# Turning two layer-norm tiles by VectorE and a trip through DRAM instead of by TensorE, at the start of an MLP

## The chip, the core and the metric

The kernel runs on one NeuronCore of a Trainium2 chip, as one launch. The metric is the device time of that launch in microseconds (us); three runs of the kernel before gave a median of 882.88 us. The core has TensorE (PE; its weight loads are shown as PEld), VectorE (DVE), ScalarE (ACT), GpSimd (POOL) and SyncE (SP), which here only issues DMAs. Each engine works through its own queue in the order in which the program was written; semaphores join the queues.

## The reference, cut to what matters

Two layers of a linear attention block followed by an MLP, on 2048 rows of 448 float32 values. Every block reads a layer-normed copy of x and adds its result to x.

```python
def _A_ref(x, wqkv, wo):          # H = 16 heads of Dh = 28
    q, k, v = split(x @ wqkv)
    phi = lambda t: where(t > 0, t + 1, exp(t)) + 1e-6
    pq, pk = phi(q), phi(k)
    kv = einsum("bhsd,bhse->bhde", pk, v);  z = sum over s of pk
    o = (pq @ kv) / (pq . z + 1e-6)
    return o @ wo
def _B_ref(x, w1, b1, w2, b2):    # F = 1792
    return gelu(x @ w1 + b1) @ w2 + b2

for layer in range(2):
    x = x + _A_ref(_layernorm(x), wqkv, wo)
    x = x + _B_ref(_layernorm(x), w1, b1, w2, b2)
```

## The kernel before, in words

The 2048 rows are 16 tiles of 128 rows; four tiles make a block (b = 0 to 3) of the MLP. Precision is kept by splitting every float32 operand into a high part in fp32r and a low part (operand minus high), so each product is three matmuls (high-high, high-low, low-high). The last 64 of the 448 columns share one chunk: its high and low weights lie in the two halves of 128 rows, which is why the last 64 columns of a normed tile are doubled before they are turned.

A layer has these stages.

- **Phase 1** goes over the 16 tiles: layer norm, turning the tile (features onto partitions), splitting, keys (`stage_k`, "psk"), the sum G of key products (`stage_g`), and queries (`stage_q`, "psq", eleven matmuls each), whose positive map is written to DRAM (`pq_d`). Queries run in phase 1 for the tiles below `DEFER`; the others are left for the next stage. Step t makes G of tile t − 1, from the keys' high and low parts kh and kl.
- **The hinge**, between the halves of the layer, is written out by hand in the string `ORDER`, one token after the other. It turns G into the matrix M = (masked kv) · wo (`kv`, `mask`, `m`, `ms`), and brings the first block through the output product: `qz`, `qs`, `tq`, `qq` prepare a tile of queries, `o` multiplies (12 matmuls, "op"), `la` adds the result to x and takes the layer-norm statistics, `lb` normalises ("xm"). Then `T` turns the normed tile by four TensorE transposes into a bank ("tp"), and `x` splits it from that bank into XH (ScalarE) and XL (VectorE). Between these stand the deferred queries: `Q` is a query's matmuls, `Qp` reads it out (two relus, "eq" and "ep", and an exponential on ScalarE, an addition on GpSimd, a store to DRAM on SyncE), and `Qv`, for the last, does the addition on VectorE. A query's result lies in one of two "h" banks, which the MLP's "hp" uses too. The token `pre` issues the four query tiles of the next block and, in layer 0 only, two pieces of the second MLP weight.
- **The MLP** goes over its four blocks with `mlp1` (11 matmuls of 512 columns, "hp", over all four tiles of a block at once), GELU, and `mlp2`; beside each block the next one is prepared as the plans PLAN_0, PLAN_1 and PLAN tell.

The first block's normed tiles are turned by TensorE. The later blocks' are turned without it: `turn` transposes 32 × 32 squares by VectorE's stream transpose into a buffer "sq" that takes two tiles, `store_sq` writes it to DRAM (512 KB), `spread` reads it back with four DMAs of 128 KB each into "sp", so that the squares end up in their places, and `split_t` splits a tile from there.

Layer norm takes statistics on VectorE (bst, bmv, bve), the inverse root on GpSimd (brs), and the normalisation on VectorE again (xm). A buffer ring "S" of five 128 × 1024 buffers holds the staged weights, the parts of M, and the squares. SyncE issues all DMAs in the order of the program text, each when its own waits are over, and what is written behind a waiting DMA waits too.

The string that orders the hinge before:

```python
    ORDER = (
        "Q ld1 z ld0 ld2 qz0 qz1 G gt qs1 Q Qp kv qs0 tq1 Q mask qz2 tq0 qs2 ld3 "
        "m0 qq1 Qp m1 qz3 ms0 qq0 m2 ms1 m3 ms2 tq2 ms3 qs3 o0 la0 qq2 o1 tq3 lb0 la1 qq3 Qp pre "
        "o2 T0 lb1 la2 o3 x0 T1 Q lb2 la3 x1 T2 Q x2 lb3 Qp "
        "T3 x3 Qp Q Qv "
    )
    DEFER = NT - ORDER.split().count("Q")
```

Of the kernel before, what the change touches and what calls it, by code (L numbers as in the profile page):

```python
# [10 lines left out]
F32R = mybir.dt.float32r  # L11
AF = mybir.ActivationFunctionType
OP = mybir.AluOpType
# [9 lines left out]
def linear_attn_mlp_kernel(  # L23
# [12 lines left out]
    pe, act, dve, pool, sp = nc.tensor, nc.scalar, nc.vector, nc.gpsimd, nc.sync  # L36
    x0 = x_in[0]
    y_out = out[0]
    S, D = x0.shape
    F = w1.shape[1]  # L40
# [4 lines left out]
    G = 112  # L45
# [10 lines left out]
    def dram(shape, dt, name):  # L56
        return tc.dram_tile(shape, dt, name=name)
# [13 lines left out]
    def t512(tag, bufs, name, dt=F32):  # L71
        return work.tile([128, 512], dt, name=name, tag=tag, bufs=bufs)

    def f(ap):
        return ap.bitcast(F32)
# [94 lines left out]
    m3 = mask.rearrange("p (h d) -> p h d", d=DH)  # L170
# [15 lines left out]
    def table(func):  # L186

        act.activation(none, tiny, func)
# [13 lines left out]
    def ln_norm(stats, name):  # L202
        xs, mv, rs = stats
        xn = t512("xn", 2, name)
        dve.tensor_scalar(xn[:, :D], xs, mv[:, 0:1], rs, op0=OP.subtract, op1=OP.mult)
        return xn
# [23 lines left out]
    def block(key):  # L230
        if key not in blocks:
            blocks[key] = Block()
        return blocks[key]
# [10 lines left out]
    def split_x(key, j):  # L244
        tp = tps.pop((key, j))
        hi, lo = blocks[key].pieces(j)
        act.copy(hi, tp)
        dve.tensor_sub(lo, tp, f(hi))
# [7 lines left out]
    def half(name):  # L256
        return work.tile([128, 1024], F32, name=name, tag="S", bufs=5)

    def turn(x, key, t):
        x = x[:, :D]  # L260
        if (key, t // 2) not in squares:
            squares[key, t // 2] = half("sq")
        sq = squares[key, t // 2].rearrange("p (m c u n) -> p c m u n", m=4, c=4, n=32)[:, :, :, t % 2]
        dve.transpose(sq[:, :3], x[:, :TL].rearrange("p (c m n) -> p c m n", c=3, n=32))
        dve.transpose(sq[:, 3].rearrange("p (u m) n -> p u m n", u=2),
                      x[:, TL:].rearrange("p (m n) -> p m n", n=32)[:, None].to_broadcast([128, 2, 2, 32]))

    def store_sq(key, h):
        d = stored[key, h] = dram([128, 1024], F32, f"sq_{'_'.join(map(str, key))}_{h}")
        sp.dma_start(d, squares.pop((key, h)))  # L270

    def spread(key, h):
        r = spreads[key, h] = half("sp")
        d = stored.pop((key, h)).rearrange("(i r) (m f) -> m r i f", i=4, m=4)
        for m in range(4):
            sp.dma_start(r[m * 32:(m + 1) * 32].rearrange("r (i f) -> r i f", i=4), d[m])

    def split_t(key, t, hi, lo):

        x = spreads[key, t // 2].rearrange("p (i c u n) -> p u c i n", i=4, c=4, n=32)[:, t % 2]  # L280
        h = hi.rearrange("p (c i n) -> p c i n", c=4, n=32)
        act.copy(h, x)  # L282
        dve.tensor_sub(lo.rearrange("p (c i n) -> p c i n", c=4, n=32), x, f(h))  # L283


    def proj(name, key, j, o=None, cs=range(4)):
# [59 lines left out]
    def background(n, m=NF):  # L346

        for g in bg_wait[:m]:
            bg_wait.pop(0)()
        for _ in range(n):  # L350
            g = next(bg, None)
            if g is not None:
                bg_wait.append(g)


    xns, split, ks = {}, {}, {}
# [79 lines left out]
    def stage_q(l, t):  # L436
        if t is None:
            return
        qo.append((l, t, proj("q", ("a", l, t // 4), t % 4)))
# [7 lines left out]
    def fill_qphi():  # L447

        l, t, o = qo.pop(0)
        e = t512("e", 3, "eq")[:, :D]  # L450
        p = t512("E", 2, "ep")[:, :D]
        act.activation(e, o, AF.Relu, scale=-1.0)
        act.activation(p, o, AF.Relu)
        act.activation(e, e, AF.Exp, scale=-1.0)
        pool.tensor_tensor(e, p, e, op=OP.add)
        sp.dma_start(pq_d[l][t * 128:(t + 1) * 128, :], e)

    def stage_g(l, t, acc):
# [14 lines left out]

    ORDER = (
# [4 lines left out]
    )  # L481
    DEFER = NT - ORDER.split().count("Q")

# [125 lines left out]
    def trans_ms(tr, g):  # L609
        if g == 0:  # L610
            tr.Mh, tr.Ml = [], []
        if g % 2 == 0:
            for n in ("Mh", "Ml"):
                s = work.tile([128, 1024], F32R, name=n, tag="S", bufs=5)
                getattr(tr, n).extend(s[:G, i * D:(i + 1) * D] for i in range(2))
        act.copy(tr.Mh[g], tr.mp[g])
        dve.tensor_sub(tr.Ml[g], tr.mp[g], f(tr.Mh[g]))

# [21 lines left out]
    def load_pq(l, b, j):  # L640
        t = b * 4 + j
        pqt[l, t] = t448(f"W{j}", 1, f"pq{l}_{t}")
        sp.dma_start(pqt[l, t], pq_d[l][t * 128:(t + 1) * 128, :])
# [64 lines left out]
    def o_n(l, b, j):  # L708
        t = b * 4 + j
        xn = xns["m", l, t] = ln_norm(sts.pop(("m", l, t)), f"xm{l}_{t}")  # L710
        if b == 0:
            act.copy(xn[:, D:], xn[:, TL:D])

    def add_bias(l, b, j):
# [5 lines left out]
        transpose_x(xn, xn[:, TL:], ("m", l, b), j)  # L720

    def m_split(l, b, j):
        split_x(("m", l, b), j)


    def q_prep(l, b, j, tr):
# [149 lines left out]
    for l in range(LAYERS):  # L876
        tr = SimpleNamespace(mp={})
        za, acc = phase1(l, tr)
        if l == 0:
            background(0)  # L880
        fill = list(range(DEFER, NT))

        def pre(j):
            for k in range(4):
                load_pq(l, 1, k)
            if l == 0:
                background(2)

        tok_ = SimpleNamespace(
            Q=lambda j: stage_q(l, fill.pop(0)), Qp=lambda j: fill_qphi(), Qv=lambda j: stage_qphi(), G=lambda j: stage_g(l, NT - 1, acc),  # L890
            ld=lambda j: (load_pq(l, 0, j), load_x(l, j)), z=lambda j: trans_z(tr, za), gt=lambda j: trans_gt(tr, acc),
            kv=lambda j: trans_kv(tr), mask=lambda j: trans_mask(tr), m=lambda j: trans_m(tr, j),
            ms=lambda j: trans_ms(tr, j), qz=lambda j: q_z(l, 0, j, tr), qs=lambda j: q_scale(l, 0, j, tr),
            tq=lambda j: q_transpose(l, 0, j), qq=lambda j: q_split(l, 0, j), o=lambda j: o_mm(l, 0, j, tr),
            la=lambda j: o_ln(l, 0, j), lb=lambda j: o_n(l, 0, j), T=lambda j: m_transpose(l, 0, j),
            x=lambda j: m_split(l, 0, j), pre=pre)
        for tok in ORDER.split():
            name, j = tok.rstrip("0123456789"), int("0" + tok.lstrip("abcdefghijklmnopqrstuvwxyzQTG"))
            getattr(tok_, name)(j)
        assert not fill and not qo  # L900
        table(AF.Gelu_apprx_tanh)
        q_z(l, 1, 0, tr)
        mlp1(l, 0, 0)
        trans_chunks(tr)
        for b in range(NB):
            acc = [bank("acc", 4, f"y{j}")[:, :D] for j in range(4)]
            nxt = b + 1 < NB
            if not nxt and l + 1 < LAYERS:
                st_k = stage_square(wqkv[:, D:2 * D])
                st_q = stage_square(wqkv[:, :D])  # L910
                load_to(l + 1, PRE - 1)
            for i in range(NF):
                if i + 1 < NF:
                    mlp1(l, b, i + 1)
                elif nxt:
                    mlp1(l, b + 1, 0)
                if l == 0 and b == 0 and i:
                    background(1, 1)
                if i == NF - 2 and not nxt and l + 1 < LAYERS:
                    table(AF.Exp)  # L920
                if 9 <= i < 13:
                    add_bias(l, b, i - 9)
                if nxt:
                    behind(l, b, i, tr)
                elif l + 1 < LAYERS:
                    if i == 2:
                        split_kq("k", st_k)
                    if i == 5:
                        split_kq("q", st_q)
                    if i in (3, 4, 6, 7, 8):  # L930
                        t = (3, 4, 6, 7, 8).index(i)
                        stage_a(l + 1, t)
                        stage_n(l + 1, t)
                        stage_t(l + 1, t)
                        if t % 2:
                            stage_sp(l + 1, t)
                    if 9 <= i < 13:
                        stage_x(l + 1, i - 9)
                mlp2(l, b, i, acc)
# [28 lines left out]
```

## Time and profile before

| what | value |
|---|---|
| median of three runs | 882.88 us (882.62 to 883.0) |
| the profiled execution: its time | 882.53 us |
| the profiled execution: its span, first to last instruction | 880.8 us |
| instructions in the span | 11686 |
| mean granted TensorE clock in the span | 1.000 |
| VectorE's stream transposes, 128 x 384 and 128 x 128 | 578 and 269 ns each |
| DMAs: HBM read and written | 55.65 MB and 34.08 MB |

The profile is one execution. The page gives the busy time of each engine and the chain of waits that ended last; the timeline gives each instruction with its start in microseconds from the first one, its duration, and in brackets the idle time before it with what ended it. TensorE's matmuls are pipelined: the pace is read from start to start, and the durations overlap. Rows of SyncE ("SPq") are issues; a DMA's landing is told separately, as the time from its issue until its semaphore is complete. The hinge of layer 0 lies at about 107 to 142 us, that of layer 1 at about 539 to 574 us.

### The profile page before, as it was taken

How to read it: one execution, taken by the hardware profiler on the slowest of the kernel's cores; microseconds unless marked ns; L12 is line 12 of the kernel's file. 1: busy time of each engine (PE TensorE's matmuls, PEld its weight loads, DVE VectorE, ACT ScalarE, POOL GpSimd, SP SyncE). 2: the span in 40 equal slices, each digit the busy share in tenths (PEclk: the TensorE clock that was granted, in tenths of full speed). 3: DMA queues.
4: the chain of work that ended last, by engine and by line, in shares of the span. 5: the costliest groups of instructions: out<-in, count | busy, mean ns of one | idle time of the engine just before them, and what ended most of it. 6: DMA issues, size and time to landing. Idle time of an engine off the chain costs nothing.

```text
span 880.8 us, 11686 instructions
## 1 busy us (share of the span) xinstructions
PE 872.7 (99%) x4190; PEld 774.4 (88%) x4190; DVE 486.2 (55%) x946; ACT 345.6 (39%) x607; POOL 219.0 (25%) x251
## 2 busy tenths in 40 slices
PE   8999999999999999999999999999999999999998
PEld 7899988888888888888899999888888888888887
DVE  6878585658455543225567866755574473432112
ACT  5577645323223232333355664442232133223221
POOL 4456632325012102011222333220220140140000
PEclk9999999999999999999999999999999999999999
DMA  6377715624413403051146452143332323110001
GB/s 177 114 214 235 217 43 170 192 81 144 132 59 102 157 0 96 1 178 48 48 133 198 150 148 95 63 158 95 103 115 90 112 74 132 48 49 34 9 1 42
DMA packets 62762, 93.71 MB, mean 106 GB/s; under 512 B 8816, under 2 KB 57968, under 8 KB 62704
## 3 DMA queue, kind: packets, MB, share of 16 engines
q1 hardware_dynamic: 62704, 92.97, 33.7%
q8 instruction: 33, 0.54, 0.3%
q14 instruction: 25, 0.20, 0.1%
HBM read 55.65 MB, written 34.08 MB: 102 GB/s over the span
## 4 chain that ended last, share of the span: by engine, by line
PE 96%; DVE 2%; ACT 1%; DMA 1%; issue 0%; SPq 0%; POOL 0%; ACTq 0%; DVEq 0%; POOLq 0%
PE y L770 10%; PE y L768 10%; PE y L769 10%; PE hp L751 9%; PE hp L750 9%; PE hp L752 9%; PE hp L754 3%; PE hp L753 3%; PE G L465 2%; PE G L466 2%; PE G L464 2%; PE psk L295 2%; PE psq L293 2%; PE psk L294 2%; PE psk L293 2%; PE psq L295 2%
## 5 line engine op out<-in xcount | busy, mean ns | idle before, releaser
L760 DVE TENSOR_TENSOR gl<-g,gh 128x512 fp32r<-128x512 f32 x112 | 82.6, 737 | 299.5 <-ACT gh L759 299.5
L756 ACT ACTIVATE g<-hp,b1s 128x512 f32<-128x512 f32 x112 | 77.0, 688 | 406.4 <-PE hp L754 406.4
L770 PE MATMUL y<-w2h,gl 128*128 128x448 f32 x448 | 163.8, 366 | 0.0
L769 PE MATMUL y<-w2l,gh 128*128 128x448 f32 x448 | 163.8, 366 | 0.0
L768 PE MATMUL y<-w2h,gh 128*128 128x448 f32 x448 | 163.7, 366 | 0.0
L751 PE MATMUL hp<-XH,w1l 128*128 128x512 f32 x336 | 131.7, 392 | 0.0
L750 PE MATMUL hp<-XH,w1h 128*128 128x512 f32 x336 | 131.3, 391 | 0.0
L752 PE MATMUL hp<-XL,w1h 128*128 128x512 f32 x336 | 131.2, 390 | 0.0
L199 POOL TENSOR_TENSOR brs<-bve,mhalf 128x1 f32<-128x1 f32 x64 | 38.9, 607 | 270.2 <-DVE bve L197 263.0
L768 PEld LDWEIGHTS y<-w2h,gh 128*128 128x128 f32 x448 | 84.2, 188 | 8.9
L769 PEld LDWEIGHTS y<-w2l,gh 128*128 128x128 f32 x448 | 84.2, 188 | 8.3
L770 PEld LDWEIGHTS y<-w2h,gl 128*128 128x128 f32 x448 | 84.3, 188 | 6.5
L752 PEld LDWEIGHTS hp<-XL,w1h 128*128 128x128 f32 x336 | 63.1, 188 | 13.5
L751 PEld LDWEIGHTS hp<-XH,w1l 128*128 128x128 f32 x336 | 63.2, 188 | 11.2
L750 PEld LDWEIGHTS hp<-XH,w1h 128*128 128x128 f32 x336 | 63.2, 188 | 11.0
L759 ACT CAST gh<-g 128x512 fp32r<-128x512 f32 x112 | 69.7, 622 | 3.6
L403 POOL TENSOR_TENSOR xnl<-x,xnh 128x384 fp32r<-128x384 f32 x32 | 35.5, 1108 | 87.7 <-ACT xnh L402 52.9
L647 POOL TENSOR_TENSOR pz<-pq,zb 128x448 f32<-128x448 f32 x32 | 36.6, 1147 | 79.5 <-DVE dn L653 70.6
L283 DVE TENSOR_TENSOR XL<-sp,XH 128x512 fp32r<-128x512 f32 x50 | 42.9, 864 | 4.7 <-ACT XH L282 4.7
L753 PE MATMUL hp<-XH,w1x 128*128 128x512 f32 x112 | 43.6, 389 | 0.0
L754 PE MATMUL hp<-XL,w1x 128*128 128x512 f32 x112 | 43.6, 389 | 0.0
L193 DVE BATCH_NORM_STATS2 bst<-x 128x6 f32<-128x448 f32 x64 | 39.9, 623 | 4.5 <-DMA x<-in_A_x_dram 3.3
(143 smaller groups left out, 1567.8 us busy)
## 6 DMA issues: line engine op xcount, KB each, us to landing
x<-in_A_x_dram SPq DMA_DIRECT2D x32, 224.0 KB, 4.1
pq_d<-eq SPq DMA_DIRECT2D x32, 224.0 KB, 2.5
pq<-pq_d SPq DMA_DIRECT2D x32, 224.0 KB, 3.3
x<-x_d SPq DMA_DIRECT2D x32, 224.0 KB, 3.4
sq_a<-sq SPq DMA_DIRECT2D x13, 512.0 KB, 2.9
sp<-sq_a SPq DMA_DIRECT2D x52, 128.0 KB, 3.1
sq_q<-sq SPq DMA_DIRECT2D x12, 512.0 KB, 2.6
sp<-sq_q SPq DMA_DIRECT2D x48, 128.0 KB, 3.0
```

The source lines that it names most:

```text
L283: dve.tensor_sub(lo.rearrange("p (c i n) -> p c i n", c=4, n=32), x, f(h))
L750: pe.matmul(o, w1h[:, c, s], x.moving(x.hi, c), start=(c == 0), stop=False)
L751: pe.matmul(o, w1l[:, c, s], x.moving(x.hi, c), start=False, stop=False)
L752: pe.matmul(o, w1h[:, c, s], x.moving(x.lo, c), start=False, stop=False)
L753: pe.matmul(o, w1x[:, s], x.moving(x.hi, 3), start=False, stop=False)
L754: pe.matmul(o, w1x[:, s], x.moving(x.lo, 3), start=False, stop=True)
L756: act.activation(g, hp, AF.Gelu_apprx_tanh, bias=b1s[:, i:i + 1])
L759: act.copy(gh, g)
L760: dve.tensor_sub(gl, g, f(gh))
L768: pe.matmul(acc[j], gh[:, s], w2h[:, i], start=first, stop=False)
L769: pe.matmul(acc[j], gh[:, s], w2l[:, i], start=False, stop=False)
L770: pe.matmul(acc[j], gl[:, s], w2h[:, i], start=False, stop=last)
```

## The change

In the first MLP block, tiles 0 and 1 are turned as the later blocks' are: VectorE transposes their squares (`tu0`, `tu1`), SyncE stores them (`st`) and reads them back (`sp`), and ScalarE splits the high part from there; the low part is GpSimd's for tile 0 and VectorE's for tile 1. Tiles 2 and 3 keep TensorE's turn. `split_t` gets the engine of its subtraction as an argument. The doubling of the last 64 columns by ScalarE stays for tiles 2 and 3 alone, since `turn` doubles them itself.

`ORDER` has seven `Q` in place of six, so `DEFER` is 9 instead of 10: the query of tile 9 leaves phase 1 and joins the hinge. In its tail `x2` stands behind `lb3`, and `x0 x1` come behind the sixth query. `ORDER` holds for both layers.

Because the ring "S" now gives two buffers to the squares here, the low parts of M's third and fourth group go into two buffers of the ring "F".

```diff
-    def split_t(key, t, hi, lo):
+    def split_t(key, t, hi, lo, eng=dve):
         x = spreads[key, t // 2].rearrange("p (i c u n) -> p u c i n", i=4, c=4, n=32)[:, t % 2]
         h = hi.rearrange("p (c i n) -> p c i n", c=4, n=32)
         act.copy(h, x)
-        dve.tensor_sub(lo.rearrange("p (c i n) -> p c i n", c=4, n=32), x, f(h))
+        eng.tensor_tensor(lo.rearrange("p (c i n) -> p c i n", c=4, n=32), x, f(h), op=OP.subtract)
...
-        "m0 qq1 Qp m1 qz3 ms0 qq0 m2 ms1 m3 ms2 tq2 ms3 qs3 o0 la0 qq2 o1 tq3 lb0 la1 qq3 Qp pre "
-        "o2 T0 lb1 la2 o3 x0 T1 Q lb2 la3 x1 T2 Q x2 lb3 Qp "
-        "T3 x3 Qp Q Qv "
+        "m0 qq1 Qp m1 qz3 ms0 qq0 m2 ms1 m3 ms2 tq2 ms3 qs3 o0 la0 qq2 o1 tq3 lb0 tu0 la1 qq3 Qp pre "
+        "o2 lb1 tu1 st la2 o3 Q sp lb2 la3 Q Qp T2 lb3 x2 Qp Q x0 x1 T3 x3 Q Qp Qv "
...
     def trans_ms(tr, g):
         if g % 2 == 0:
-            for n in ("Mh", "Ml"):
+            for n in ("Mh", "Ml")[:1 if g else 2]:
                 s = work.tile([128, 1024], F32R, name=n, tag="S", bufs=5)
                 getattr(tr, n).extend(s[:G, i * D:(i + 1) * D] for i in range(2))
+        if g >= 2:
+            tr.Ml.append(t512("F", 2, "Ml", F32R)[:G, :D])
...
     def o_n(l, b, j):
         xn = xns["m", l, t] = ln_norm(sts.pop(("m", l, t)), f"xm{l}_{t}")
-        if b == 0:
+        if b == 0 and j >= 2:
             act.copy(xn[:, D:], xn[:, TL:D])
...
     def m_split(l, b, j):
-        split_x(("m", l, b), j)
+        if j < 2:
+            split_t(("m", l, b), j, *block(("m", l, b)).pieces(j), dve if j else pool)
+        else:
+            split_x(("m", l, b), j)
...
+            tu=lambda j: turn(xns.pop(("m", l, j)), ("m", l, 0), j),
+            st=lambda j: store_sq(("m", l, 0), 0), sp=lambda j: spread(("m", l, 0), 0), pre=pre)
```

The functions that the new tokens call, unchanged:

```python
    def turn(x, key, t):
        x = x[:, :D]
        if (key, t // 2) not in squares:
            squares[key, t // 2] = half("sq")
        sq = squares[key, t // 2].rearrange("p (m c u n) -> p c m u n", m=4, c=4, n=32)[:, :, :, t % 2]
        dve.transpose(sq[:, :3], x[:, :TL].rearrange("p (c m n) -> p c m n", c=3, n=32))
        dve.transpose(sq[:, 3].rearrange("p (u m) n -> p u m n", u=2),
                      x[:, TL:].rearrange("p (m n) -> p m n", n=32)[:, None].to_broadcast([128, 2, 2, 32]))

    def store_sq(key, h):
        d = stored[key, h] = dram([128, 1024], F32, f"sq_{'_'.join(map(str, key))}_{h}")
        sp.dma_start(d, squares.pop((key, h)))

    def spread(key, h):
        r = spreads[key, h] = half("sp")
        d = stored.pop((key, h)).rearrange("(i r) (m f) -> m r i f", i=4, m=4)
        for m in range(4):
            sp.dma_start(r[m * 32:(m + 1) * 32].rearrange("r (i f) -> r i f", i=4), d[m])
```

More of the change, by code (lines that the diff above doesn't have):

```diff
@@ L895, in linear_attn_mlp_kernel @@
             la=lambda j: o_ln(l, 0, j), lb=lambda j: o_n(l, 0, j), T=lambda j: m_transpose(l, 0, j),
-            x=lambda j: m_split(l, 0, j), pre=pre)
+            x=lambda j: m_split(l, 0, j), tu=lambda j: turn(xns.pop(("m", l, j)), ("m", l, 0), j),
+            st=lambda j: store_sq(("m", l, 0), 0), sp=lambda j: spread(("m", l, 0), 0), pre=pre)
         for tok in ORDER.split():
```

## The prediction

> **What bounds the kernel now.** I read the page first: the busy shares and the shares of the chain of waits.
>
> ```profile
> PE 872.7 (99%) x4190; PEld 774.4 (88%) x4190; DVE 486.2 (55%) x946; ACT 345.6 (39%) x607; POOL 219.0 (25%) x251
> PE 96%; DVE 2%; ACT 1%; DMA 1%; issue 0%; SPq 0%; POOL 0%; ACTq 0%; DVEq 0%; POOLq 0%
> ```
>
> TensorE is the bound nearly everywhere, so work taken from it is gained at once, and a wait given to it is lost at once. Next the timeline of TensorE in the first layer's hinge (the stretch that ORDER lays out), the second layer's first MLP matmul, and, from the table of waits, the one wait that TensorE has there. Columns: start, duration, engine, line, instruction.
>
> ```profile
> 110.47 0.37 PE L293 MATMUL psq<-wq,XH 128*128 128x448 f32 x1
> ...
> 112.69 3.31 PE L596 MATMUL kvp<-gt,stg 128*112 128x112 f32 x32
> ...
> 130.25 0.60 PE L242 MATMUL tp<-ident,xm 128*128 128x128 f32 x4
> 130.61 0.45 PE L685 MATMUL op<-Mh,qh 112*128 112x448 f32 x1
> 130.89 0.36 PE L686 MATMUL op<-Ml,qh 112*128 112x448 f32 x1
> ...
> 141.78 0.39 PE L750 MATMUL hp<-XH,w1h 128*128 128x512 f32 x1
> 573.52 0.39 PE L750 MATMUL hp<-XH,w1h 128*128 128x512 f32 x1
> PE psq L293 <- ACT ep L453: 0.7, 2, 0.4
> ```
>
> One query is eleven matmuls, 112.69 − 110.47 = 2.22 us, 0.20 each. A tile's turn by TensorE is 130.61 − 130.25 = 0.36, and the matmul behind it steps 0.28 instead of 0.20: 0.44 in all. The MLP begins at 141.78 and 573.52; the last query waits 0.35 in each layer for a bank that ScalarE still reads.
>
> **What goes.** Four turns (two tiles, two layers): 4 × 0.44 = 1.76 us of TensorE, and at best the two waits, 0.7. ScalarE loses two 64-column copies a layer, which cost nothing while it waits there. One query moves from phase 1 into the hinge: 2.22 leave phase 1 and return, 0 where both places are TensorE's. Is phase 1 TensorE's without it? The low half of the ninth step's keys (kl) must be ready when G's second matmul comes. VectorE's rows and TensorE's, layer 0 and then layer 1:
>
> ```profile
> 78.09 0.58 DVE L264 STREAM_TRANSPOSE sq<-x 128x384 f32<-128x384 f32 x1
> 78.60 0.27 DVE L265 STREAM_TRANSPOSE sq<-x 128x128 f32<-128x128 f32 x1
> 78.79 0.58 DVE L427 SCALAR_TENSOR_TENSOR kl<-psk,kh 128x448 fp32r<-128x448 f32 x1
> 80.94 0.37 PE L465 MATMUL G<-kl,xnh 128*128 128x448 f32 x1
> 509.23 0.59 DVE L427 SCALAR_TENSOR_TENSOR kl<-psk,kh 128x448 fp32r<-128x448 f32 x1
> 512.74 0.36 PE L465 MATMUL G<-kl,xnh 128*128 128x448 f32 x1
> ```
>
> The query removed stands ahead of that matmul. Layer 0: 80.94 − 2.22 = 78.72, but kl ends at 79.37, so TensorE waits 0.65, say 0.7, and phase 1 gains 1.5. (Bounds: 0 if VectorE catches up, 1.2 if the next step waits half as long again.) Layer 1: 510.52 against 509.82: no wait, 2.22 gained.
>
> **What comes: the trip through DRAM.** Tiles 0 and 1 are turned by VectorE (tu0, tu1), stored (st), read back by four DMAs (sp) and split (x0 by ScalarE and GpSimd, x1 by ScalarE and VectorE). ScalarE's queue has x0, x1, then the split of tile 3 and the last two queries' readings; the MLP's first matmul needs the high halves of all four tiles, and the bank that the sixth query's reading frees. So if the spread is late, everything is. When does it land? First the turning. VectorE and GpSimd at the end of the first output tiles:
>
> ```profile
> 127.42 0.51 DVE L205 TENSOR_SCALAR xm<-x,bmv,brs 128x448 f32<-128x448 f32 x1
> 127.85 0.62 DVE L705 TENSOR_TENSOR x<-op,x 128x448 f32<-128x448 f32 x1
> ...
> 129.61 0.55 POOL L199 TENSOR_TENSOR brs<-bve,mhalf 128x1 f32<-128x1 f32 x1 [2.23 <-DVE bve L197]
> 130.13 1.15 POOL L455 TENSOR_TENSOR eq<-ep,eq 128x448 f32<-128x448 f32 x1
> ```
>
> tu0 stands between these two VectorE instructions: it waits for xm to end (127.93, plus 0.03 as at 78.09), then 0.70 (78.09 to 78.79): the addition starts at 128.66, 0.81 late. It feeds tile 1's statistics, whose brs on GpSimd is queued ahead of the third query's addition (eq), which thereby goes from 130.13 to 130.94 too. That addition is what SyncE's queue stands on. SyncE's own rows, layer 0 and layer 1:
>
> ```profile
> 131.31 0.32 SPq L456 DMA_DIRECT2D pq_d<-eq  x1
> 131.73 1.83 SPq L643 DMA_DIRECT2D pq<-pq_d  x4
> 133.61 0.90 SPq L336 DMA_DIRECT2D stg<-in_B_w_dram  x2
> ...
> 563.10 0.32 SPq L456 DMA_DIRECT2D pq_d<-eq  x1
> 563.52 1.84 SPq L643 DMA_DIRECT2D pq<-pq_d  x4
> ```
>
> The new store is written behind these ("pre" precedes "st"): not at the end of tu1, near 133, but at 134.51 + 0.81 + 0.04 = 135.36 in layer 0 (four loads and two weight pieces ahead) and 565.36 + 0.85 = 566.21 in layer 1 (no weight pieces). How long does it take behind such a burst? Landing times of the burst's own: weight pieces of layer 0, then the four loads of layer 1; below them a store in a burst of phase 1, then a store and spread with a free queue, and that spread's landing:
>
> ```profile
> DMA to landing us min/median/max: 4.1/4.1/4.2
> DMA to landing us min/median/max: 2.6/3.3/3.8
> 51.88 0.38 SPq L270 DMA_DIRECT2D sq_a<-sq  x1
> DMA to landing us min/median/max: 4.7/4.7/4.7
> 254.53 0.33 SPq L270 DMA_DIRECT2D sq_m<-sq  x1
> 257.56 1.75 SPq L276 DMA_DIRECT2D sp<-sq_m  x4
> DMA to landing us min/median/max: 2.6/3.0/3.1
> ```
>
> With a free queue the store takes at most 257.56 − 254.53 = 3.0; in a burst up to 4.7. I take the burst's last latencies with 0.1 for the larger store, 4.2 and 3.9. From landing to spread landed: 0.05, plus 1.75 − 0.43 to the last issue, plus 3.1: 4.47. So the spread is there at 135.36 + 4.2 + 4.47 = 144.03 and 566.21 + 3.9 + 4.47 = 574.58.
>
> The Trainium skill ("DMA: Bandwidth & Descriptors", section "Anatomy of one DMA") puts a DMA at about 2.0 us plus its bytes at 436 GB/s, a fit for the path that GpSimd issues; its estimate here would be 3.2 for the store and 2.3 for a spread, the two trips 1.8 and 1.5 shorter, and the kernel near 884.1.
>
> Then ScalarE. Its rows at the hinge's end, and one VectorE subtraction:
>
> ```profile
> 139.75 0.59 ACT L247 CAST XH<-tp 128x512 fp32r<-128x512 f32 x1
> 140.21 0.57 ACT L452 ACTIVATE eq<-psq 128x448 f32<-128x448 f32 x1
> 140.65 0.57 ACT L453 ACTIVATE ep<-psq 128x448 f32<-128x448 f32 x1
> 140.37 0.69 DVE L248 TENSOR_TENSOR XL<-tp,XH 128x512 fp32r<-128x512 f32 x1 [2.19 <-ACT XH L247]
> ```
>
> x0, x1, x3 at a step of 0.46, relu 0.44, ep 0.57, plus 0.04: 2.43 until the bank is free. The MLP starts at 146.5 and 577.0. GpSimd's subtraction over 512 columns appears nowhere; 1.15 × 512/448 = 1.31 from its row over 448. It ends 0.59 + 1.31 = 1.90 after x0 starts; if it holds VectorE off, two subtractions of 0.69 follow, 3.28, against 2.43 for the bank. So it costs 0 to 0.85 a layer; I take 0, because the low half is wanted only by the MLP's third matmul and VectorE's subtraction may also run beside it.
>
> **The sum.** Layer 0: 146.5 − 141.78 = 4.7, less 1.5 from phase 1: +3.2. Layer 1: 577.0 − 573.52 = 3.5, less 2.22: +1.3. Together +4.5, on the profiled execution's 882.53: 887.0. The 1.76 is not subtracted: TensorE is then waiting, and what it has saved only lengthens that wait. The median of the runs, 882.88, lies 0.35 above the profiled one: 887.4. Behind the hinge nothing more is late: the table load, first GELU and the chunk DMAs follow the same ScalarE and SyncE queues at the same distance from the MLP's start.
>
> **Rivals.**
> *The store is not held by the loads ahead of it* (3.0 and 2.9 instead of 4.2 and 3.9), as with the free queue: 2.2 less, 885.2; with no wait in phase 1, 884.5. For it: the loads issue over 1.8 us, so the queue may be nearly drained. Against: the growth from 2.6 to 3.8 within those four.
>
> *The trip is hidden, and the kernel is faster.* That takes the spread in SBUF before TensorE ends the seventh query. TensorE would reach the MLP at 141.78 − 0.88 − 0.35 + 2.22 = 142.8; ScalarE needs 2.4 of it, so the spread must land by 140.4, the store be issued by about 133. The gain would be 1.76 + 0.7 − 0.7: 881.1. Against it stand the issues that SyncE has in front of st. It decides in each half alone; one half hidden and the other late comes out near no change.
>
> *TensorE's clock falls in the wait.* TensorE idles from 142.8 to 146.5, 3.7 us, and 2.5 in layer 1. The table of stretches at the end of the run, and the first matmuls of the run:
>
> ```profile
> 877.00:878.00 1.00, 0.21 (x2) 0.00 (x0) 0.94 (x2) 0.00 (x0) 0.00 (x0) 1.00 0.97 364
> 880.00:880.80 0.80, 0.00 (x0) 0.00 (x0) 0.00 (x0) 0.00 (x0) 0.00 (x0) 0.83 0.00 0
> 1.11 5.06 PE L157 MATMUL warm<-ones 128*128 128x128 f32 x22 [1.11 <-DVE ones L152]
> ```
>
> The last matmul ends at 877.21, and the granted clock is down some 3.3 us later. The warm-up matmuls then bound the price: 0.23 each, so at most half of 5.06 is lost, 2.5: 889.9, or 892.4 in both layers. The Trainium skill ("TensorE: Matmul & The Clock Gate", section "Part 1: The HAM clock gate") says that an idle window of about 3.4 us halves the clock; by that rule layer 0 is at the edge, and the trace's 3.3 agrees.
>
> **How the numbers follow.** Forecast 0.60; store not held 0.17; clock 0.13; hidden in both halves 0.06; one half hidden, about no change, 0.04. About 0.2%, 1.8 us, is what a measurement of this kernel can tell from none: the first three are all slower by more, so slower 0.90, same 0.04, faster 0.06. The range reaches down to the store not held (884.5) and up to the forecast with a store at 4.7 (+1.3) and a subtraction that holds both layers by 0.85 (+1.7), 890.4, and the clock's 889.9, or part of both: 891.0.
>
> **What would show it.** In the profile after: the sq_m store of the hinge issued at about 2 us behind tu1's last transpose; its landing about 4 us later; a wait of ScalarE for "sp" and one of TensorE for ScalarE's "ep" (or XH) ahead of the first hp in both layers, 2 to 4 us each; G waiting for kl some 0.7 once in layer 0. A TensorE without a wait ahead of hp, or a store that goes out before the loads, would prove the forecast wrong.

## The result and the profile after

The changed kernel takes 897.53 us (median of five runs, 897.21 to 900.47) beside 882.75 for the kernel before (five runs, 882.04 to 883.0): a ratio of 1.0173, interval 1.0161 to 1.0184. It is slower, as forecast, but by 14.8 us where 4.5 were forecast, and above the end of the range, 891.0. The profiled execution took 897.53 us with a span of 895.8 us; before, 882.53 and 880.8.

The page of the kernel after: busy time by engine, the chain's shares, and the granted clock in 40 slices.

```profile
PE 876.3 (98%) x4174; PEld 773.9 (86%) x4174; DVE 490.1 (55%) x950; ACT 344.7 (38%) x605; POOL 224.8 (25%) x255
PEclk9999998999999999999999999999999999999999
PE 88%; DMA 5%; DVE 3%; ACT 1%; issue 1%; SPq 1%; POOL 1%; ACTq 0%; DVEq 0%; POOLq 0%
```

TensorE has 16 matmul rows less and yet 3.6 us more busy time, and its share of the chain falls from 96% to 88%. DMA stands in the chain with 5%, and the clock row has an 8 in the slice that holds the first hinge. The table of TensorE's waits names the place (total, times, longest):

```profile
PE hp L756 <- ACT ep L453: 8.8, 2, 5.3
...
PE G L465 <- DVE kl L427: 1.1, 2, 0.9
```

The first matmul of the MLP waits 5.3 us in layer 0 and 3.5 in layer 1. The timeline of the kernel after, SyncE's queue, ScalarE and TensorE, layer 0 and then layer 1:

```profile
132.03 0.32 SPq L456 DMA_DIRECT2D pq_d<-eq  x1
132.45 1.83 SPq L645 DMA_DIRECT2D pq<-pq_d  x4
134.34 0.90 SPq L336 DMA_DIRECT2D stg<-in_B_w_dram  x2
135.33 0.38 SPq L270 DMA_DIRECT2D sq_m<-sq  x1
142.00 1.75 SPq L276 DMA_DIRECT2D sp<-sq_m  x4
146.45 1.14 ACT L282 CAST XH<-sp 128x512 fp32r<-128x512 f32 x2 [4.80 <-DMA sp<-sq_m]
149.00 0.80 PE L756 MATMUL hp<-XH,w1h 128*128 128x512 f32 x1 [5.28 <-ACT ep L453]
...
573.69 0.42 SPq L270 DMA_DIRECT2D sq_m<-sq  x1
579.34 1.74 SPq L276 DMA_DIRECT2D sp<-sq_m  x4
586.55 0.50 PE L756 MATMUL hp<-XH,w1h 128*128 128x512 f32 x1 [3.47 <-ACT ep L453]
```

The number in brackets is the idle time before an instruction and what ended it. Read the list from the top. The store of the squares goes out at 135.33, 0.03 from the forecast. SyncE waits for it to land before it issues the spread at 142.00: 6.7 us later. From the first issue of the spread to ScalarE's cast it is 4.45, where the forecast had 4.47, and from the cast to hp it is 2.55. In layer 1 the store takes 5.6. The table of DMA issues has it in a row each (KB, then us to landing), a row per layer:

```profile
sq_m<-sq SPq DMA_DIRECT2D x1, 512.0 KB, 6.7
...
sq_m<-sq SPq DMA_DIRECT2D x1, 512.0 KB, 5.6
```

What follows the wait is in the table of stretches (start and end, length, busy time of PE, PEld, DVE, ACT and POOL, granted clock, DMA share, GB/s):

```profile
147.00:149.00 2.00, 0.00 (x0) 0.00 (x1) 1.38 (x2) 2.00 (x6) 1.26 (x1) 0.58 0.00 0
149.00:152.00 3.00, 3.00 (x7) 2.40 (x8) 1.18 (x2) 2.91 (x5) 2.26 (x2) 0.50 0.14 54
152.00:154.00 2.00, 2.00 (x6) 1.54 (x6) 0.00 (x0) 0.00 (x0) 0.00 (x0) 0.50 0.79 264
154.00:156.00 2.00, 2.00 (x10) 1.66 (x9) 0.48 (x1) 1.31 (x2) 0.00 (x0) 0.97 0.63 191
...
589.00:591.00 2.00, 2.00 (x6) 1.54 (x6) 0.00 (x0) 0.51 (x2) 0.36 (x1) 0.50 0.56 209
```

In both hinges the granted clock fell to 0.50 and TensorE worked at that clock for about five and three and a half microseconds: six matmuls in 2 us instead of ten.

The experiments are easiest to read by stretches of the program. The table gives the change of each against the kernel before, in us of the profiled execution, worked out from the start times in the timeline: of the first kvp matmul (112.69 and 544.51 before), the first hp (141.78 and 573.52), the first G of layer 1 (451.99) and the end (880.8). "Phase 1" of layer 0 counts from the span's start. The ratio is that of the timed runs against the kernel before on the same chip, with its interval.

| kernel | ratio | phase 1, l. 0 | hinge, l. 0 | MLP, l. 0 | phase 1, l. 1 | hinge, l. 1 | rest |
|---|---|---|---|---|---|---|---|
| after | 1.0173 (1.0161 to 1.0184) | −0.1 | +7.3 | +2.5 | −2.2 | +5.5 | +1.9 |
| e1_loads_last | 1.0037 (1.0023 to 1.0050) | −0.7 | +2.4 | +1.4 | −0.6 | +2.4 | +0.2 |
| e2_store_first | 1.0059 (1.0044 to 1.0074) | −2.2 | +4.9 | +1.7 | −2.3 | +3.7 | +0.3 |
| e3_warm | 1.0130 (1.0116 to 1.0144) | −1.3 | +7.1 | +0.1 | −2.2 | +7.2 | +0.1 |
| e4_seven | 1.0011 (1.0001 to 1.0021) | −0.4 | +2.1 | 0.0 | −2.3 | +2.2 | 0.0 |
| e5_no_pieces | 1.0136 (1.0123 to 1.0150) | −1.8 | +5.7 | +1.6 | −0.6 | +5.2 | +2.7 |
| e6_loads_behind_eq | 1.0032 (1.0020 to 1.0045) | −1.9 | +2.4 | +0.6 | −2.3 | +2.5 | +0.2 |
| e7_gap_at_7 | 1.0022 (1.0014 to 1.0031) | −1.3 | +2.4 | +0.2 | −2.3 | +2.4 | +0.2 |
| e8_six | 1.0055 (1.0039 to 1.0070) | +0.3 | +1.5 | +1.1 | 0.0 | +1.5 | +1.1 |
| e9_cast_on_dve | 1.0030 (1.0019 to 1.0040) | −0.6 | +1.9 | +1.0 | −0.6 | +1.9 | +1.3 |
| e10_store_by_act | 1.0046 (1.0030 to 1.0061) | −1.1 | +3.6 | +0.3 | −2.2 | +3.2 | +0.3 |
| e11_subs_on_dve | 1.0024 (1.0013 to 1.0036) | −1.2 | +1.9 | +0.9 | −2.2 | +1.9 | +1.1 |

Two of the columns also move for reasons other than the edits. Layer 0's phase 1 depends, in most of the traces, on when the spread of tile 10's squares lands, which moves from run to run. Layer 1's phase 1 shows −2.2 or −2.3 where a query was taken out of it (e8 takes out none), except in e1, e5 and e9, where TensorE's matmuls of that stretch took 368 ns instead of 365, at a granted clock that the profile gives as 1.00; that costs 1.6 us.

### The profile page after: what moved, and what is told of

Same layout as the page of the kernel before. It is cut to its first block, busy times and chain, and to the rows that moved or that the text cites. A ratio compares the mean times of both kernels' runs of the same rounds, so it can differ in the third digit from the quotient of the medians.

```text
span 895.8 us, 11678 instructions
## 1 busy us (share of the span) xinstructions
PE 876.3 (98%) x4174; PEld 773.9 (86%) x4174; DVE 490.1 (55%) x950; ACT 344.7 (38%) x605; POOL 224.8 (25%) x255
## 4 chain that ended last, share of the span: by engine, by line
PE 88%; DMA 5%; DVE 3%; ACT 1%; issue 1%; SPq 1%; POOL 1%; ACTq 0%; DVEq 0%; POOLq 0%
PE y L776 10%; PE y L774 10%; PE y L775 10%; PE hp L756 9%; PE hp L757 9%; PE hp L758 9%; PE hp L760 3%; PE hp L759 3%; PE G L465 2%; PE G L466 2%; PE G L464 2%; PE op L699 2%; PE psk L295 2%; PE op L698 2%; PE op L700 2%; PE psk L294 2%
## 5 line engine op out<-in xcount | busy, mean ns | idle before, releaser
L283 DVE TENSOR_TENSOR XL<-sp,XH 128x512 fp32r<-128x512 f32 x52 | 45.6, 883 | 17.1 <-ACT XH L282 17.1
```

Source lines behind the costliest of these rows:

```text
L283: eng.tensor_tensor(lo.rearrange("p (c i n) -> p c i n", c=4, n=32), x, f(h), op=OP.subtract)
```

## The experiments

**e1_loads_last: the six loads behind the spread.** Theory: the store is late because it stands behind the loads that "pre" issues.

```
-... qq3 Qp pre o2 lb1 tu1 st la2 o3 Q sp lb2 ...
+... qq3 Qp o2 lb1 tu1 st la2 o3 Q sp pre lb2 ...
```

> The changed kernel with one token moved: pre (four query loads, and in layer 0 two weight pieces) stands behind sp instead of ahead of st, so the squares' store and spread meet an empty DMA queue. Theory 1, the trip is late because its store drains behind the burst of loads (6.66 and 5.63 us to landing after): the store goes out at tu1's end, near 133, lands in about 3.0, the spread is in SBUF by 140.5; TensorE's wait ahead of hp (5.3 and 3.6 us) shrinks to under 0.6 in both layers, the clock stays at 1.00, and the time falls by about 13: 882 to 884.5 us. Theory 2, the trip is too long by itself: the store still lands after 4 us or more, TensorE waits 2 us or more ahead of hp, 888 us or more.

Measured: 886.50 us beside 883.06. The DMA rows of e1, layer 0 and then layer 1:

```profile
sq_m<-sq SPq DMA_DIRECT2D x1, 512.0 KB, 2.6
...
sq_m<-sq SPq DMA_DIRECT2D x1, 512.0 KB, 2.6
```

The same store, with none of the loads ahead of it, lands in 2.6 us. The wait ahead of hp is 0.3 us in layer 0 and 0.4 in layer 1, the clock stays at 1.00 throughout, and some 11 of the 14.8 us are gone. So the place of the loads in the queue, six in layer 0 and four in layer 1, is what most of the loss hangs on. The store and the waits came out as theory 1 had them, but the time did not: it lies between the two theories. About 3.4 us are left, and part of them is new: in the chain of waits of e1 stand a store of phi(q), now behind the loads, and an hp matmul that waits for it at one remove.

```profile
140.13 5.04 DMA pq_d<-eq
...
147.17 0.50 PE hp L756
```

**e2_store_first: the loads between the store and the spread.**

```
-... qq3 Qp pre o2 lb1 tu1 st la2 o3 Q sp ...
+... qq3 Qp o2 lb1 tu1 st pre la2 o3 Q sp ...
```

> The changed kernel with pre between st and sp: the store is ahead of the loads, the spread behind them. If a DMA waits for the bytes queued ahead of it (six loads of 224 KB took 5.8 us to drain before), the store lands in about 3 us, but the spread lands some 1 to 2 us later than with the loads last, TensorE waits 1 to 2.5 us ahead of hp in each layer, short of the 3.3 us at which the clock falls: 885 to 888 us. If only the store is sensitive (its place in the queue, or writes behind reads), the result is that of the loads-last kernel, within 1 us.

Measured: 888.63 us beside 883.06. The store lands in 3.0 us, but now the spread stands behind the loads and pays instead:

```profile
sq_m<-sq SPq DMA_DIRECT2D x1, 512.0 KB, 3.0
sp<-sq_m SPq DMA_DIRECT2D x4, 128.0 KB, 6.0
```

hp waits 2.9 us in layer 0. The expectation took such a wait to be too short for the clock, but it halved there (0.51 in this row of e2's stretches), which makes up the +1.7 under "MLP":

```profile
146.00:148.00 2.00, 2.00 (x6) 1.61 (x5) 0.62 (x1) 1.47 (x2) 1.32 (x2) 0.51 0.47 176
```

Whatever stands behind the loads is late, be it one store of 512 KB or four loads of 128 KB.

**e3_warm: TensorE kept busy through the wait.** Twenty-four matmuls of 128 columns on a constant stand behind the last query, for their activity alone; nothing reads their result. The timeline shows each of them as two rows, and they take 5.5 us, not the 2.8 that were expected.

```
-... T3 x3 Q Qp Qv
+... T3 x3 Q kw Qp Qv
+    def keep_warm(n):
+        keep = bank("m", 2, "keep")
+        for i in range(n):
+            pe.matmul(keep[:, :128], ones, ones, start=True, stop=True)
```

> The changed kernel with 24 matmuls on a constant (128 columns, float32, about 2.8 us) behind the seventh query in each layer, inside TensorE's wait; they go to a bank that nobody reads. If the halved clock after the wait comes from the idle time, the clock stays at 1.00 through both hinges, hp's first matmuls step 0.23 and not 0.46, and the time falls by the 2.51 + 1.94 us by which TensorE slips behind the first hp: about 893.1 us. If the clock is halved for another reason, or costs nothing, 897 us or more.

Measured: 895.11 us beside 883.06. Timeline of e3 at layer 0's hinge, and a row of its stretches:

```profile
142.33 5.52 PE L753 MATMUL keep<-ones 128*128 128x128 f32 x48
146.38 0.55 ACT L452 ACTIVATE eq<-psq 128x448 f32<-128x448 f32 x1
147.61 0.48 PE L761 MATMUL hp<-XH,w1h 128*128 128x512 f32 x1
```

```profile
147.00:150.00 3.00, 3.00 (x18) 2.49 (x17) 1.60 (x3) 2.95 (x5) 2.03 (x2) 1.00 0.01 4
```

The hinges are about as long as in the kernel after (layer 0) or longer (layer 1), but the clock stays at 1.00 and the columns behind hp fall from +2.5 and +1.9 to +0.1 and +0.1. So some 4.2 of those 4.4 us are the clock's, and it fell because TensorE stood idle. Only part of it is won, since in layer 1 the 5.5 us of extra matmuls outlast the wait of 3.5 that they fill.

**e4_seven: the kernel before, with the seventh query alone.** Tiles 0 and 1 are still turned by TensorE.

```
-o2 T0 lb1 la2 o3 x0 T1 Q lb2 la3 x1 T2 Q x2 lb3 Qp T3 x3 Qp Q Qv
+o2 T0 lb1 la2 o3 x0 Q T1 Q lb2 la3 x1 Qp T2 Q x2 lb3 Qp T3 x3 Qp Q Qv
```

> The kernel before (TensorE turns all four tiles) with a seventh query in the hinge and nothing else: the query of tile 9 leaves phase 1. If phase 1 is TensorE's without it, nothing changes: 882.8 us. The prediction's step (kl late by 0.7 in layer 0) gives 883.5. What the trace after shows, no gain at all in phase 1 of layer 0 (G at the end of phase 1 is 0.1 later, not 2.2 earlier), would give about 885.0, the 2.2 us of the query in the hinge unpaid in layer 0 alone.

Measured: 884.17 us beside 883.06, 0.1% more, between the last two of the expected times. A query costs the hinge 2.1 to 2.2 us and gives phase 1 of layer 1 2.3 us back. In layer 0 it gives back less, 0.4 us in this profile. Moving the query thus costs about 1 us and is a small part of the loss.

**e5_no_pieces: two of the six loads moved.** The two weight pieces of layer 0 go behind the spread, so that layer 0 has four loads ahead of the store, as layer 1 has.

```
         def pre(j):
             for k in range(4):
                 load_pq(l, 1, k)
-            if l == 0:
-                background(2)
...
-... o3 Q sp lb2 ...
+... o3 Q sp bw lb2 ...        (bw: background(2) in layer 0)
```

> The changed kernel with the two weight pieces of layer 0 (458 KB of the 1376 KB that are issued ahead of the squares' store) issued behind the spread; the four loads of phi(q) stay ahead. Queue theory (the store lands late because its transfer stands behind the loads'): in layer 0 the store lands in about 5.6 us as it does in layer 1, where four loads stand ahead of it, instead of 6.66; hp waits some 4.2 us instead of 5.3, the clock still halves, 896.4 us. Rival (landing has its own fixed time here, or layer 0's was chance): 6.7 us again and 897.5 us. Layer 1 as before in both.

Measured: 894.49 us beside 882.53. The DMA rows of e5, layer 0 and layer 1:

```profile
sq_m<-sq SPq DMA_DIRECT2D x1, 512.0 KB, 6.0
...
sq_m<-sq SPq DMA_DIRECT2D x1, 512.0 KB, 5.5
```

Layer 0's 6.0 us lies between the two expectations. It does not show that fewer loads make the store land sooner, for in e3_warm, which leaves all six loads ahead of the store, layer 0's store took the same:

```profile
sq_m<-sq SPq DMA_DIRECT2D x1, 512.0 KB, 6.0
```

So 6.7 and 6.0 us are a spread between runs with the same six loads, and the rival, that part of layer 0's 6.7 was chance, stays open. What e5 does show is that four loads are enough for a landing of 5.5 to 6.0 us. Its store also goes out earlier, since SyncE need not issue the two pieces first, which takes 1.0 us. hp waited 3.7 and 3.2 us, the clock still fell in both layers, and the time is 2 us under the queue theory's.

**e10_store_by_act: the same order, but the store issued by ScalarE's queue.**

```
-        sp.dma_start(d, squares.pop((key, h)))
+        (act if key[0] == "m" and key[2] == 0 else sp).dma_start(d, squares.pop((key, h)))
```

> The changed kernel with the squares' store of MLP block 0 issued by ACT's queue, not SP's; the six or four loads ahead stay on SP. If the store is late because it stands in the same queue (first come, first served within it): on its own queue it lands in about 2.6 to 3.2 us as when nothing is ahead, hp waits some 1.5 to 2 us, the clock stays, 889 us. If it is late because all queues share the 16 DMA engines, which are busy with the loads: 5.5 to 6.7 us as now, hp waits 5 and 3.5 us, 896 to 898 us. ACT's issue holds it for 0.3 to 0.4 us in both.

Measured: 887.16 us beside 883.16; the loads stay where they were. The DMA rows of e10, layer 0 and layer 1:

```profile
sq_m<-sq ACTq DMA_DIRECT2D x1, 512.0 KB, 4.2
...
sq_m<-sq ACTq DMA_DIRECT2D x1, 512.0 KB, 4.6
```

The landing falls between the two theories and says that both hold in part; the time is under both. The store also goes out earlier, at 132.04 in layer 0, because it no longer waits for SyncE to issue six loads. The packets of the store in the traces, 128 of 4096 bytes, show two parts of the lateness. In e1 the first starts 0.8 us after the issue, and all are through 1.4 us later. In the kernel after they move between those of the loads: the first starts 2.6 us after the issue in layer 0 and 2.1 in layer 1, and they take 3.5 and 3.2 us. In e10 the first starts after 1.7 and 1.3 us, and they take 2.1 and 2.9. hp waits 1.6 and 1.1 us, and the clock does not fall. The Trainium skill ("DMA: Bandwidth & Descriptors", section "Queues, rings and completion order") says that SyncE and ScalarE each own a row of rings on the same 16 DMA engines, that an engine consumes a ring in order and takes the rows in turn; the three landings, 2.6, 4.2 to 4.6 and 5.6 to 6.7, agree with that.

**e6_loads_behind_eq: the loads behind the next store of phi(q) as well.** From here the question is whether the change can pay at all.

```
-... o3 Q sp pre lb2 la3 Q Qp T2 ...        (e1)
+... o3 Q sp lb2 la3 Q Qp pre T2 ...
```

> As e1_loads_last, but the loads stand behind the next query's phi(q) store too. In e1 that store of layer 0 was issued behind the loads (140.13 us) and landed in 5.04 us; the buffer that it held was waited for by ACT's eq at 145.2, and hp's second bank by 0.9 us behind that. If that wait was the queue's doing, it goes: 0.9 to 1.3 us off e1, 885.4 us. Rival (the store is late for the squares' spread ahead of it, or the bank is late for VectorE's last query anyway): 886.5 us as e1.

Measured: 885.68 us, 884.02 to 886.6, beside 882.53. In the profile the wait of 0.9 us that e1 had behind hp is gone, and the column "MLP" falls from +1.4 to +0.6. By the medians nothing can be told from e1 (1.0032 beside 1.0037). TensorE's last two waits, 0.5 and 0.4 us in each layer, are for ScalarE. Its timeline in e6, ahead of hp at 142.28; the spread had landed at 138.27:

```profile
138.39 0.55 ACT L452 ACTIVATE eq<-psq 128x448 f32<-128x448 f32 x1
138.83 0.55 ACT L453 ACTIVATE ep<-psq 128x448 f32<-128x448 f32 x1
139.25 0.59 ACT L454 ACTIVATE eq<-eq 128x448 f32<-128x448 f32 x1
139.72 1.15 ACT L282 CAST XH<-sp 128x512 fp32r<-128x512 f32 x2
140.75 0.60 ACT L247 CAST XH<-tp 128x512 fp32r<-128x512 f32 x1
141.22 0.57 ACT L452 ACTIVATE eq<-psq 128x448 f32<-128x448 f32 x1
141.66 0.57 ACT L453 ACTIVATE ep<-psq 128x448 f32<-128x448 f32 x1
```

No gap anywhere: the two casts of the spread come into the last four microseconds, with the work on tile 3 and the last queries. In the kernel before, XH of tiles 0 and 1 was made at 131.72 and 134.56, behind idle times of 1.5 and 2.1 us:

```profile
131.56 0.25 ACT L712 COPY xm<-xm 128x64 f32<-128x64 f32 x1 [1.52 <-DVE xm L205]
131.72 0.58 ACT L247 CAST XH<-tp 128x512 fp32r<-128x512 f32 x1
134.40 0.24 ACT L712 COPY xm<-xm 128x64 f32<-128x64 f32 x1 [2.11 <-DVE xm L205]
134.56 0.58 ACT L247 CAST XH<-tp 128x512 fp32r<-128x512 f32 x1
```

**e7_gap_at_7: layer 0's phase 1 leaves out another step's query.**

```
-                elif tok == "Q" and t < DEFER:
-                    stage_q(l, t)
+                elif tok == "Q" and (t < DEFER if l else t < 7 or 8 <= t < 10):
+                    stage_q(l, t if l or t < 7 else t - 1)
```

> As e6_loads_behind_eq, and in layer 0's phase 1 step 7 is the one without a query, not step 9 (queries of tiles 7 and 8 at steps 8 and 9). Layer 0's phase 1 had got 0 to 1.9 us of the 2.2 us of a query shorter in five traces, because XH of tile 10 came late for the spread (landed in the short step 8) and kl behind it. Theory: with step 8 at full length the spread has its time, phase 1 keeps 2 us of gain, 884.2 us. Rival (VectorE's work bounds steps 8 to 10 however the queries lie): as e6, 885.4 us, or the wait only moves two steps ahead.

Measured: 884.92 us beside 882.53. Phase 1 of layer 0 gained 1.3 us in the profile, where e6 gained 1.9; G waited 0.8 us for kl at a later step. In this profile the wait only moved, as the rival had it; the time, 884.92, lies between the two expectations and does not decide.

**e8_six: e1 with six queries in the hinge.** Only the turning by squares is left of the change.

```
-... la3 Q Qp T2 lb3 x2 Qp Q x0 x1 T3 x3 Q Qp Qv
+... la3 Q Qp T2 lb3 x2 Qp x0 x1 T3 x3 Q Qv
```

> As e1_loads_last with six queries between the halves, not seven (ten in phase 1, as before the change): only the turning by squares is left of the change. Theory (the trip through DRAM is 8 us or so and the queries only cover it): hp waits about 2.3 us longer in each layer and phase 1 gets 0.5 to 2.2 us longer while the hinge loses a query of 2.3: 888 to 890 us, with the clock halved where hp waits over 3.4 us, then some 2 us more. Rival (the seventh query is what costs): under 885 us.

Measured: 887.40 us beside 882.53, just under the theory's 888 to 890 and over the rival's 885. So the seventh query does cover something: by the medians e8 is 1.4 us slower against the kernel before than e1, which is less than the query's own 2.2. The waits of TensorE in e8:

```profile
PE tp L242 <- DVE xm L205: 3.1, 2, 1.6
PE hp L756 <- ACT XH L247: 1.4, 2, 0.7
PE hp L758 <- POOL XL L283: 1.3, 2, 0.7
```

With a query less TensorE reaches the turn of tile 3 before VectorE has normalized that tile and waits 1.5 to 1.6 us a layer there, and 1.3 more in two pieces behind it.

**e9_cast_on_dve and e11_subs_on_dve: the spread's casts on VectorE, then GpSimd's subtraction too.** Both start from e6.

```
     def split_t(key, t, hi, lo, eng=dve):
...
-        act.copy(h, x)
+        if key[0] == "m" and key[2] == 0:
+            dve.tensor_copy(h, x)
+        else:
+            act.copy(h, x)
...
-            split_t(("m", l, b), j, *block(("m", l, b)).pieces(j), dve if j else pool)
+            split_t(("m", l, b), j, *block(("m", l, b)).pieces(j), dve)        (e11 only)
```

> As e6_loads_behind_eq, but the two XH casts of the spread squares run on VectorE, not on ACT. In e6 ACT ran without a gap from 137.76 us to hp's start (two tail copies and casts of turned tiles, eq, ep, the spread's two casts of 1.15 us, XH of tile 3, eq, ep), the spread had landed at 138.27, VectorE stood idle 1.7 us, and both last waits of PE (psq 0.5 and hp 0.37 us) were for ACT's ep. Theory (with the trip covered, ACT's order is the last bound of the hinge): both waits go, 0.5 to 0.8 us a layer, 1.0 to 1.6 us off e6: 884.3 us by medians, a span of 881. Rival (VectorE gets late instead: XL of tiles 0 or 3 is waited for): 885.7 us or more. Neither is under the kernel before by more than 0.2%.

> As e9_cast_on_dve, but the XL of tile 1 is made by VectorE too (0.69 us there, 1.74 us beside VectorE on POOL, where it stood behind an eq of 1.16 us). In e9 hp started without a wait but its third matmul waited 0.54 us for that XL in layer 0 and 0.52 in layer 1. Theory: VectorE had 1.9 us idle after its XL of tile 3, so the wait goes and nothing takes its place: 1.0 us off e9 when phase 1 and the rest are the same, 884.5 to 885 us, 0.1 to 0.25% over the kernel before. Rival (VectorE's XL of tile 3, now 0.7 us later, is waited for instead): 886 us.

Measured: 886.12 us beside 883.16, and 885.76 beside 884.16. In both the first matmul of hp no longer waits, and in both its third does. The waits of e9, and under them those of e11:

```profile
PE hp L761 <- POOL XL L286: 1.1, 2, 0.5
```

```profile
PE hp L761 <- DVE XL L248: 1.1, 2, 0.5
```

With ScalarE relieved, TensorE waits for GpSimd's low half, that of tile 0 (e11's expectation calls it tile 1's). With GpSimd relieved, it waits for VectorE's low half of tile 3, which the spread's work now stands ahead of. Both times the gain stayed away, as the rival had it: in e11 for the rival's reason, in e9 for another engine, since its rival had named VectorE. In none of the versions is the kernel faster than before.

## Why the prediction was wrong

**What held.** The place, the chain and the order were as forecast: SyncE issues the store behind the loads (135.33, forecast 135.36), the addition on VectorE goes 0.8 us late (128.60, forecast 128.66), the spread takes 4.45 us (4.47), then ScalarE's three casts and two readings, then hp. Layer 1's phase 1 gained 2.23 us (2.22). GpSimd's subtraction over 512 columns took 1.26 us (1.31) and held nothing up. The last query's wait stayed (0.45 us a layer), as the sum assumed, and TensorE's saved turns only lengthened its wait.

**The term that was mis-sized: the store's landing.** The forecast took the latencies of the burst's last loads in the kernel before, 4.1 and 3.8 us, and added 0.1 for the store's size: 4.2 and 3.9. Measured were 6.7 and 5.6: 2.5 and 1.7 us more, all of it on the path. The step that failed is the transfer of the landing time of a queue's last member to one that comes behind it. Such a latency holds what stood ahead of that member. For the next one the member's own bytes come on top, and those of the store itself: 512 KB, more than two loads of 224 KB. That is the argument; that the place behind the loads makes the store late is shown by e1 (2.6 us with no loads ahead), e2 (the lateness moves to whatever stands behind) and e10 (4.2 and 4.6 beside the loads instead of behind them). How much of it goes with the bytes is not shown: six loads ahead gave 6.7 us and 6.0, four gave 5.5 to 6.0. e10 comes near the case that the forecast had in mind, though not as a clean test (its store goes out earlier, its spread meets the loads in layer 0 and takes 4.1 to 4.4 us instead of 3.1): with landings of 4.2 and 4.6 the hinges lengthen by 3.6 and 3.2 us, where 4.7 and 3.5 were forecast, and the whole by 4.0, where 4.5 was. The rival "not held by the loads" looked for the error on the wrong side. The Trainium skill's estimate for the store, 3.2 us ("DMA: Bandwidth & Descriptors", section "Anatomy of one DMA"), is for one DMA alone, so e1's 2.6 and e2's 3.0 are what to hold it against, and not the 6.7 and 5.6 of this queue.

**The rival that came on top: the clock.** It had a chance of 0.13, priced at 2.5 a layer, because the forecast wait of 3.7 us lay at the edge. With the store late by more, the wait was 5.3 and 3.5 us, and the clock halved in both layers: +2.5 and +1.9, which e3 takes away. The price was about right, though not the bound that it was called: e5's layer 1 lost 2.7. The chance was too low even for the forecast's own wait: in these runs the clock halved with each wait of 2.9 us or more (2.9, 3.2, 3.5, 3.7, 5.3) and with none of 1.6 or less. The prediction read 3.3 us between the last matmul and the clock's fall from the end of one run. At the ends of the thirteen profiled runs that time goes from 2.1 to 5.2 us, and in the waits themselves from 1.9 to 4.6. In e10, whose last matmul ends at 881.37, the clock falls within this stretch:

```profile
883.00:884.00 1.00, 0.00 (x0) 0.00 (x0) 0.00 (x0) 0.00 (x0) 0.00 (x0) 0.72 0.60 228
```

So 3.3 us was one draw and no threshold, and not even the forecast's 2.5 us in layer 1 was known to be safe: no wait between 1.6 and 2.9 us was measured. The halved clock was tied to the store's landing as well, and not a case apart from it.

**The third piece.** Layer 0's phase 1 gained nothing in this profile, where 1.5 was forecast. The experiments that leave out the same step's query scatter around the forecast, 0.4 to 2.2; here ScalarE's cast of tile 10 waited 2.55 us for a spread (1.19 before), and kl was late by 0.9 us behind it.

**The ledger**, in us of the profiled execution: 4.5 forecast, 2.5 and 1.7 for the landings, 2.5 and 1.9 for the clock, 1.5 for phase 1, are 14.6 of the 15.0 by which it is slower. The rest, 0.4, is made of small differences such as ScalarE's stretch from the cast to hp, 2.55 in layer 0 where 2.43 was taken.

**Would it have paid with the trip hidden?** The forecast put that at 881.1. e1, e6, e7, e9 and e11 hide the trip, and none is under the kernel before: ratios of 1.0022 to 1.0037. Part of the answer is that the turns were worth less than the 1.76 us that the forecast took. From start to start, the transposes of a hinge take 1.67 us of TensorE before and 0.95 in e6 and e11, 0.7 less for two tiles, while the matmuls of the output product ("op") take 10.0 to 10.1 before and 10.2 to 10.3 there. That leaves some 0.5 us a layer, 1.0 in all. The rest is waits: the two casts and two subtractions of tiles 0 and 1 (1.15 us on ScalarE, 0.69 on VectorE, 1.7 on GpSimd in e6) now come at the hinge's end, where all three engines have the work of tile 3 and the last queries. Of e6, e9 and e11 each took away the wait that it was built for, and another engine's stood in its place: 0.4 for ScalarE's ep, 0.5 for GpSimd's low half, 0.5 for VectorE's. That this crowding at the end accounts for all of the loss is argued from these waits and not shown. What stays open is the last microsecond or two: the runs of one version scatter by 2 to 4 us, and no order of the three engines was found that brings it below the kernel before.

## What to carry to other kernels

A DMA's time to landing depends on its place in the queue. A latency read from the trace counts for the DMA that has it. One put behind it lands later, by 1.7 and 2.5 us more than was allowed for here, so it is better put ahead of the bulk loads, or on another queue. A wait of TensorE that comes near 3 us should be priced with a halved clock behind it, 1.6 to 2.7 us here, and an error in the wait can bring that price in. Work taken from the busiest engine is only gained if what replaces it arrives while the other engines still have gaps; work that arrives at the end of a stretch meets everything else that ends there.

## What the hardware showed that had not been expected

- The store's landing had three levels for the same 512 KB: 2.6 us with no loads ahead (2.9 and 3.0 with the loads issued right behind it), 4.2 to 4.6 beside the loads on another queue, 5.5 to 6.7 behind four or six loads of 224 KB on the same queue.
- The loads ahead took longer too: in the kernel after, layer 0's two weight pieces took 5.7 us (5.2 in e3_warm), where those of the kernel before took 4.1 and 4.2 without the store behind them. No run isolates the cause. The row of the kernel after:

```profile
stg<-in_B_w_dram SPq DMA_DIRECT2D x2, 224.0 KB, 5.7
```

- Waits of 2.9 and 3.2 us were enough to halve the clock. The clock's own records in the traces put the halved stretches of the kernel after at 147.31 to 154.13 and 587.63 to 591.04, 6.83 and 3.41 us long; the one of e2 is 3.41 long, those of e5 3.41 and 6.83. In layer 1 of the kernel after the clock had fallen only 1.1 us after hp began. The Trainium skill ("TensorE: Matmul & The Clock Gate", section "Part 1: The HAM clock gate") says that an idle window of about 3.4 us halves it and about 3.4 us of work bring it back, with a window that runs freely. The lengths of 3.41 and twice that agree; the waits of 2.9 and 3.2 us are shorter than such a window.
- In e11 the two identical casts on VectorE took 0.42 and 1.38 us; the second ran beside an addition of GpSimd, which itself took 1.37 us where 1.15 is usual. Rows of e11:

```profile
139.79 0.42 DVE L283 CAST XH<-sp 128x512 fp32r<-128x512 f32 x1
140.85 1.38 DVE L283 CAST XH<-sp 128x512 fp32r<-128x512 f32 x1
140.57 1.37 POOL L458 TENSOR_TENSOR eq<-ep,eq 128x448 f32<-128x448 f32 x1 [2.44 <-ACT eq L457]
```

- In three of the thirteen profiles (e1, e5, e9) the matmuls of layer 1's phase 1 took 368 ns instead of 365, and its steps 6.82 us instead of 6.69, at a granted clock of 1.00: 1.6 us over the stretch. No run tells why.
